# Logits in pairs of blocks, one issue for a chunk's four output products, and a new order of the work

## Chip, core and metric

The kernel runs on one core of a Trainium2 chip. The metric is the device time of one execution in microseconds (us). The kernel before takes 249.48 us, the median of three runs (248.29 to 249.7).

## What is computed

Two stages in fp32. `x` is [4, 11456, 128], `inducing` [32, 128]; the second stage has 8 experts of 4 slots each, 32 slots in all, and a hidden width of 1024.

```python
def mab(q, kv):
    s = scale * (q @ kv.transpose(0, 2, 1))
    s = s - s.max(-1, keepdims=True)
    a = np.exp(s)
    a /= a.sum(-1, keepdims=True) + 1e-09
    return a @ kv
h = mab(I, x)
x = mab(x, h)
...
logits = x @ phi
d = np.exp(logits - logits.max(0, keepdims=True))
d /= d.sum(0, keepdims=True) + 1e-09
slot_input = d.T @ x
...
h = np.maximum(slot_input[e] @ w1[e], 0.0)
slot_out[e] = h @ w2[e]
...
c = np.exp(logits - logits.max(1, keepdims=True))
c /= c.sum(1, keepdims=True) + 1e-09
return c @ slot_out
```

The maxima of `d` run over all 45824 rows of a slot, those of `c` over the 32 slots of a row.

## The kernel before

The rows of a batch are laid out as 128 partitions by 90 blocks, and a **chunk** is 15 blocks: 6 chunks for each of 4 batches, 24 in all (`n` or `a`, 0 to 23). A chunk's working tile is 128 x 480: for each partition, 15 blocks of 32 values. All of the program is a list of steps, each with an engine and a function. A table of numbers, `ORDER`, written out by hand, says in which order the steps are issued; each engine then works through its own in that order and waits where an input or a buffer isn't ready. Costs beside the steps play no part in the running program.

For each chunk the steps are:

- **First pass** (`first_scores`, `first_sum`): TensorE makes the scores `s1p` (L301), VectorE takes a maximum (L312), ScalarE the exponential (L359), VectorE transposes blocks (L362), TensorE sums `ha` (L378). After six chunks a batch's `h` follows from it (`first_out`).
- **Second pass** (`second`): TensorE makes `s2p` (L301), VectorE transposes (L544) and takes row maxima (L547), GpSimd subtracts (L551), ScalarE takes exp (L554), TensorE transposes (`tt`, L560), ScalarE copies (L565, L567), TensorE makes the logits with their row sums, `lp` (L573). VectorE adds 1e-9 to the sums (L582), inverts them (L583) and writes the scaled logits into `l_all` (`ble`, L589); for the last chunk of a batch ScalarE writes the fifteenth block (`blf`, L592). GpSimd scales the weights (L596). `l_all` holds one block after another, 32 slots side by side.
- **Slot maxima** (`segment`, three chunks each, eight segments): for segments 0, 2, 3, 4 and 5 VectorE takes the maximum over three chunks at once (`t`, L630), for the others over one chunk at a time (`tm`, L618). Both walk along the blocks of one slot, 32 values apart. TensorE, VectorE (`mc`, L642), TensorE (`pb`, L645) and ScalarE (`m_all`, L648) spread it over the partitions; GpSimd subtracts it (`d`, L667), ScalarE takes exp (L671), and TensorE adds a chunk's 15 small products to `u` (L680), which ScalarE copies out (L689).
- **Experts** (`experts`): joins the segments (L732 to L757), from which the products `sip` (L748), `sit`, `hpm`, `so` and in the end the matrix `srs` (L844) follow.
- **Third pass** (`third`, with `soft`): row maximum `cm` (VectorE, L483), subtraction `ct` (GpSimd, L487), exp (ScalarE, L491), row sum `cz` (VectorE, L508; where the chunk is in `CHALF`, GpSimd first adds two halves, L499), 1e-9 added (L511, GpSimd for the 18 chunks in `CEP`, VectorE for six), reciprocal (VectorE, L514), scaling (GpSimd, L889), and a transpose back into `l_all` (VectorE, L892). It needs only the logits, so it may run ahead of `srs`; `ct` has three buffers.
- **Output** (`output`): four products for each chunk, one for each group of 32 partitions (L922), each into a bank of its own, taken from six that go round (`mm`); the other two banks belong to `ha` and `u`. ScalarE or VectorE copies each product out (L936), and SyncE's queue stores a chunk (L944).

SyncE's queue also loads `x` in 960 KB pieces into 13 buffers, and at the end the weights.

Of the kernel before, what the change touches and what calls it, by code (L numbers as in the profile page):

```python
# [13 lines left out]
S = 32  # L14
# [14 lines left out]
SZ = S + 1  # L29

# [43 lines left out]

# [973 lines left out]
```

## Time and profile before

| | |
|---|---|
| median of three runs | 249.48 us |
| the profiled execution | 249.23 us |
| its span in the trace | 247.2 us |
| TensorE busy | 206.3 us, 83% |
| VectorE busy | 170.2 us, 69% |
| ScalarE busy | 127.6 us, 52% |
| GpSimd busy | 132.8 us, 54% |
| DMA | 73.86 MB; 23.59 MB of it written |
| mean granted TensorE clock | 0.848 of full |

The span is what the trace covers from the first instruction to the last; the execution's own time is 2.0 us longer. In the rows below PE is TensorE (PEld its weight loads), DVE VectorE, ACT ScalarE, POOL GpSimd, and L12 is line 12 of the kernel. Busy time says how long an engine had an instruction in work, and the idle time before an instruction is put down to what came last.

### The profile page before, as it was taken

The page shows a single profiled execution, that of the slowest core. Times are in us where ns is not written, and L with a number is a line of the kernel's source. Part 1 is how long each engine was busy: PE and PEld are TensorE (multiplying, and loading weights), DVE is VectorE, ACT ScalarE, POOL GpSimd, SP SyncE. Part 2 cuts the span into 40 slices and gives each one's busy share as a digit, 9 for nine tenths or more (in the row PEclk, how much of TensorE's full clock was granted, in tenths as well). Part 3 has the DMA queues.
Part 4 walks back from the last instruction along what each step waited for, and adds up shares of the span by engine and source line. Part 5 has one row for each costly group of instructions (what it writes and reads, how often), then busy time and mean ns, then how long its engine had stood idle before and what let it go on. Part 6 is the DMA issues. An engine that isn't in the chain of part 4 may idle for free.

```text
span 247.2 us, 6831 instructions
## 1 busy us (share of the span) xinstructions
PE 206.3 (83%) x2762; PEld 134.0 (54%) x2762; DVE 170.2 (69%) x389; ACT 127.6 (52%) x307; POOL 132.8 (54%) x155
## 2 busy tenths in 40 slices
PE   7699999999999889979999847898999993849300
PEld 7465654964569753658738737784555460313000
DVE  0123859989999989999999991278895556473400
ACT  3478416662468623767348443035994586545310
POOL 0000004775879569959599889738366126673100
PEclk9999999999999999999999975599995556555555
DMA  7999999979999999939993000001997649297697
GB/s 225 405 427 415 333 414 423 417 326 333 424 418 421 419 416 417 417 111 392 423 419 125 3 0 3 4 3 70 381 416 310 260 179 418 113 415 308 251 401 303
DMA packets 13134, 73.86 MB, mean 299 GB/s; under 512 B 1712, under 2 KB 3376, under 8 KB 13104
## 3 DMA queue, kind: packets, MB, share of 16 engines
q1 hardware_dynamic: 12672, 73.27, 73.4%
q8 instruction: 21, 0.34, 0.6%
q10 hardware_dynamic: 432, 0.17, 0.2%
q14 instruction: 9, 0.07, 0.1%
HBM read 49.84 MB, written 23.59 MB: 297 GB/s over the span
## 4 chain that ended last, share of the span: by engine, by line
PE 50%; DVE 29%; issue 4%; DMA 4%; POOL 4%; ACT 3%; SPq 1%; POOLq 0%; ACTq 0%; DVEq 0%
PE po L922 20%; PE ha L378 7%; PE lp L573 4%; PE s1p L301 4%; DMA xn<-xn 4%; DVE bt L544 4%; DVE tm L618 3%; DVE l_all L589 3%; DVE bm L547 3%; PE tp L278 3%; DVE t L630 3%; DVE l_all L892 3%; PE hpm L802 2%; PE s2p L301 2%; DVE s L312 2%
## 5 line engine op out<-in xcount | busy, mean ns | idle before, releaser
L922 PE MATMUL po<-l_all,srs 32*128 32x480 f32 x192 | 52.2, 872 | 13.0 <-DVE l_all L892 9.8
L936 ACT COPY ot<-po 128x480 f32<-128x480 f32 x71 | 36.3, 568 | 24.3 <-PE po L922 23.6
L922 PEld LDWEIGHTS po<-l_all,srs 32*128 32x128 f32 x192 | 26.1, 258 | 37.8 <-ACT ot L936 18.5
L487 POOL TENSOR_TENSOR ct<-l_all,cm 128x480 f32<-128x480 f32 x24 | 23.8, 995 | 19.5 <-DVE l_all L892 19.2
L551 POOL TENSOR_TENSOR bt<-bt,bm 128x480 f32<-128x480 f32 x24 | 23.6, 998 | 14.5 <-DVE bm L547 12.9
L667 POOL TENSOR_TENSOR d<-l_all,m_all 128x480 f32<-128x480 f32 x24 | 28.7, 1212 | 3.0 <-ACT m_all L648 2.7
L596 POOL TENSOR_TENSOR bt<-bt,bz 128x480 f32<-128x480 f32 x24 | 23.8, 998 | 11.8 <-DVE bz L583 4.8
L936 DVE COPY ot<-po 128x480 f32<-128x480 f32 x25 | 16.0, 646 | 19.7 <-PE po L922 19.7
L889 POOL TENSOR_TENSOR ct<-ct,cz 128x480 f32<-128x480 f32 x24 | 23.8, 996 | 7.8 <-DVE cz L514 3.9
L312 DVE TENSOR_SCALAR_CACHE_REDUCE s<-s1p 128x480 f32<-128x480 f32 (+1 forms) x24 | 15.2, 638 | 16.4 <-PE s1p L301 16.4
L573 PE MATMUL lp<-bdg,a2t 128*128 128x132 f32 x192 | 26.3, 281 | 0.0
L573 PEld LDWEIGHTS lp<-bdg,a2t 128*128 128x128 f32 x192 | 23.4, 190 | 3.7 <-issue 1.8
L378 PE MATMUL ha<-xn,e 128*32 128x128 f32 x570 | 19.8, 275 | 1.8 <-issue 0.9
L301 PE MATMUL s1p<-xt,it_sb 128*32 128x480 f32 x160 | 19.7, 573 | 1.6 <-ACT xt L286 1.1
L671 ACT ACTIVATE d<-d 128x480 f32<-128x480 f32 x24 | 14.3, 605 | 12.9 <-POOL d L667 12.8
L554 ACT ACTIVATE bt<-bt 128x480 f32<-128x480 f32 x24 | 14.3, 604 | 12.5 <-POOL bt L551 12.3
L301 PE MATMUL s2p<-xt,hts 128*32 128x480 f32 x160 | 19.2, 570 | 0.0
L359 ACT ACTIVATE s<-s,negm 128x480 f32<-128x480 f32 (+1 forms) x24 | 16.4, 692 | 5.1 <-DVE negm L343 5.0
L378 PEld LDWEIGHTS ha<-xn,e 128*32 128x32 f32 x570 | 16.0, 109 | 4.3 <-issue 1.7
L491 ACT ACTIVATE ct<-ct 128x480 f32<-128x480 f32 x24 | 14.6, 613 | 5.9 <-POOL ct L487 5.9
L508 DVE TENSOR_REDUCE cz<-ct 128x15 f32<-128x480 f32 x22 | 13.8, 634 | 5.3 <-ACT ct L491 5.3
L892 DVE STREAM_TRANSPOSE l_all<-ct 128x480 f32<-128x480 f32 x24 | 15.7, 664 | 1.6 <-POOL ct L889 1.5
(123 smaller groups left out, 346.7 us busy)
## 6 DMA issues: line engine op xcount, KB each, us to landing
xn<-xn SPq DMA_DIRECT2D x19, 960.0 KB, 10.1
out<-ot SPq DMA_DIRECT2D x19, 960.0 KB, 5.7
xt<-xt SPq DMA_DIRECT2D x14, 960.0 KB, 15.1
w<-w SPq DMA_DIRECT2D x8, 960.0 KB, 8.1
l_all<-xn SPq DMA_DIRECT2D x4, 960.0 KB, 11.5
l_all<-xt SPq DMA_DIRECT2D x4, 960.0 KB, 5.9
out<-ot SPq DMA_DIRECT2D x12, 240.0 KB, 2.5
out<-ot SPq DMA_DIRECT2D x4, 480.0 KB, 5.5
```

Of the source, the lines that this page charges most:

```text
L301: nc.tensor.matmul(dst[32 * g : 32 * g + 32, :w], lhs, src, start=True, stop=True)
L312: nc.vector.tensor_scalar(t[:, :v], T["s1p", a][:, :v], 1.0, None, op0=ALU.mult, op1=ALU.max, accum_out=m6[:, a : a + 1])
L378: nc.tensor.matmul(ha[32 * q : 32 * q + 32, :P], T["e1", a][:, j * S : (j + 1) * S], T["xn", a][:, j * P : (j + 1) * P], start=c == lo and ...
L487: nc.gpsimd.tensor_tensor(blocks(t), blocks(src()), T[mk][:, :nb].unsqueeze(2).broadcast_to(full), op=ALU.subtract)
L551: nc.gpsimd.tensor_tensor(t, t, T["bm", n][:, :nb].unsqueeze(2).broadcast_to(full), op=ALU.subtract)
L573: nc.tensor.matmul(pt[:, q * 4 * SZ : (q * 4 + m) * SZ], t[: m * S, q * P : (q + 1) * P], bdgs[b % 2].rearrange("p q s -> p (q s)")[: m * ...
L596: nc.gpsimd.tensor_tensor(t, t, T["bz", n][:, :nb].unsqueeze(2).broadcast_to(full), op=ALU.mult)
L667: e.tensor_tensor(blocks(t), blocks(l_of(n)), m.unsqueeze(1).broadcast_to([P, nb, S]), op=ALU.subtract)
L889: nc.gpsimd.tensor_tensor(t, t, T["cz", n][:, :nb].unsqueeze(2).broadcast_to([P, nb, S]), op=ALU.mult)
L892: nc.vector.transpose(l_of(n), T[ck][:, :w])
L922: nc.tensor.matmul(ptile(banks[g], po[g])[:, :w], T["srs",][q, :], l_of(n)[q, :], start=True, stop=True)
L936: (nc.vector.tensor_copy if dve else nc.scalar.copy)(ot[:, g * w : (g + 1) * w], T["po", m][:, :w])
```

## The change

**Layout.** `l_all` gives each chunk 16 blocks instead of 15 (`LW` = 512 values), in pairs: the two blocks of a pair lie value by value beside each other, so the two values of one slot are neighbours. The sixteenth block is written with the fifteenth, as its copy. The slot maxima walk over neighbours, then 64 values on to the next pair. What reads or writes single blocks (`ble`, `cm`, most of `ct`) now steps by two values. `blf` runs for all 24 chunks, and `ble` covers 14 blocks.

```diff
 def l_of(n):
-    o = STARTS[n % NCH] * S
-    return l_all[:, n // NCH, o : o + width(n)]
+    return l_all[:, n * LW : n * LW + width(n)]
+def l_pairs(n):
+    return l_all[:, n * LW : (n + 1) * LW].rearrange("p (a s e) -> p a s e", s=S, e=2)
+def l_blocks(n):
+    return l_pairs(n).rearrange("p a s e -> p a e s")
+def l_slots(n, m=1):
+    return l_all[:, n * LW : (n + m) * LW].rearrange("p (a s e) -> p s a e", s=S, e=2)
...
 def mx():
-    nc.vector.tensor_reduce(stile(pre + "m", mk, JM, RINGS[pre + "m"])[:, :nb], blocks(src()), axis=AX.X, op=ALU.max)
+    m = stile(pre + "m", mk, LW // S, RINGS[pre + "m"])
+    nc.vector.tensor_reduce(m.rearrange("p (a e) -> p a e", e=2), l_blocks(n), axis=AX.X, op=ALU.max)
...
-m = nb - (1 if valid(n) < w else 0)
+m = nb - 1
 def ble():
-    z = T["bz", n][:, :m].unsqueeze(2).broadcast_to([P, m, S])
-    nc.vector.tensor_tensor(blocks(l_of(n))[:, :m], lz()[:, :m, :S], z, op=ALU.mult)
+    z = T["bz", n][:, :m].rearrange("p (a e) -> p a e", e=2).unsqueeze(3).broadcast_to([P, m // 2, 2, S])
+    x = lz()[:, :m, :S].rearrange("p (a e) s -> p a e s", e=2)
+    nc.vector.tensor_tensor(l_blocks(n)[:, : m // 2], x, z, op=ALU.mult)
 def blf():
-    nc.scalar.activation(l_of(n)[:, m * S :], lz()[:, m, :S], AF.Identity, scale=T["bz", n][:, m:nb], bias=far)
+    x = lz()[:, m, :S].unsqueeze(2).broadcast_to([P, S, 2])
+    if valid(n) < w:
+        nc.scalar.activation(l_pairs(n)[:, m // 2], x, AF.Identity, scale=T["bz", n][:, m:nb], bias=far)
+    else:
+        nc.scalar.mul(l_pairs(n)[:, m // 2], x, T["bz", n][:, m:nb])
...
-nc.vector.tensor_reduce(T["tm", k][:, i * S : (i + 1) * S], by_slot(l_of(n)), axis=AX.X, op=ALU.max)
+nc.vector.tensor_reduce(T["tm", k][:, i * S : (i + 1) * S], l_slots(n), axis=AX.XY, op=ALU.max)
...
-nc.vector.tensor_reduce(stile("t1", ("t1", k), S, 4), by_slot(l), axis=AX.X, op=ALU.max)
+nc.vector.tensor_reduce(stile("t1", ("t1", k), S, 2), l_slots(ns[0], seg), axis=AX.XY, op=ALU.max)
```

`ds` (the difference `d`) keeps the pairs, and the small products then read `d` in steps of two, except for the four chunks in `DW`, where `ds` itself writes block by block.

**Small steps on other engines.** Both additions of 1e-9 go to ScalarE: 24 times `bze` (from L582) and 24 times `ep` (from L511; `CEP` goes away). Four chunks are subtracted on VectorE instead of GpSimd (`DV = [12, 20, 21, 23]`), and four sums are halved on GpSimd instead of two (`CHALF = [9, 10, 11, 16]`).

```diff
+def bze():
+    nc.scalar.activation(stile("bz", ("bz", n), JM, RINGS["bz"])[:, :nb], lz()[:, :, S], AF.Identity, bias=eps)
 def ep():
-    (nc.gpsimd if slow else nc.vector).tensor_scalar_add(T[zk][:, :nb], T[zk][:, :nb], 1e-9)
+    nc.scalar.activation(T[zk][:, :nb], T[zk][:, :nb], AF.Identity, bias=eps)
```

**Output.** All eight banks go round in one ring (`mm`: 8), and the four products of a chunk are one step of the list. Of the 96 copies VectorE makes 29 instead of 25.

```diff
+def mm():
+    btile("x", ("ot", n))
+    for g in range(4):
+        q = slice(32 * g, 32 * g + 32)
+        nc.tensor.matmul(ptile("mm", ("po", 4 * n + g))[:, :w], T["srs",][q, :], l_of(n)[q, :], start=True, stop=True)
```

**Order.** `ORDER` is a new table throughout, and the costs written beside the steps are other numbers:

```diff
-    "000102030405060e070a08090p0b0c0f0d0h0g0A0l0i0j0q0k0w0m0s0r0u0L0t0n0v0x0B0o0D0C0F0E0W0y0G0H0z0M0I0O170N180Q3o0P0S0J0R0T0X0K0Z0Y113s101319120U1a141f3p0V1i3w1g151l1j3t163q1h3A1b3u1k1c"
+    "000102030406050e07080a090b0p0c0f0d0l0g0h0A0j0i0k0q0m0w0r0s0u0L0t0n0v0x0B0o0D0C0F0E0W0H0G0y0I0M0z0S0N0Q173z180O0J0P0R0X0K0T0Z0Y113D101319120U1a1f3A0V143H1i1g151l1j1h163B1k3L1b1m3E1c"
```

Three places of it. GpSimd ahead of the experts (`d_18` is the difference of chunk 18, `mb` the tile of the joined segments, `bt` a chunk's weights), before:

```order
L667 TENSOR_TENSOR d_18_2269<-l_all_78,m_all_79 128x480
L667 TENSOR_TENSOR d_19_2274<-l_all_78,m_all_79 128x480
L735 TENSOR_TENSOR mb_2214<-m_all_79 128x224
L667 TENSOR_TENSOR d_20_2306<-l_all_78,m_all_79 128x480
L667 TENSOR_TENSOR d_21_2329<-l_all_78,m_all_79 128x480
L667 TENSOR_TENSOR d_22_2351<-l_all_78,m_all_79 128x480
L743 TENSOR_TENSOR mb_2214<-us_all_82,mb_2214 128x224
```

Three differences of chunks 18 to 20 and two of the last segment stand around the two steps on `mb`. GpSimd at the same place now:

```order
L691 TENSOR_TENSOR d_15_2205<-l_all_78,m_all_79 128x512
L691 TENSOR_TENSOR d_16_2220<-l_all_78,m_all_79 128x512
L691 TENSOR_TENSOR d_17_2235<-l_all_78,m_all_79 128x512
L691 TENSOR_TENSOR d_18_2278<-l_all_78,m_all_79 128x512
L691 TENSOR_TENSOR d_19_2300<-l_all_78,m_all_79 128x512
L759 TENSOR_TENSOR mb_2079<-m_all_79 128x224
L620 TENSOR_TENSOR bt_22_2096<-bt_22_2096,bz_22_2222 128x480
L620 TENSOR_TENSOR bt_21_2057<-bt_21_2057,bz_21_2208 128x480
L767 TENSOR_TENSOR mb_2079<-us_all_82,mb_2079 128x224
```

The difference of chunk 20 has left GpSimd for VectorE, and the three of chunks 15 to 17 have come in; two scalings of weights stand between the two steps on `mb`, and chunk 21's and 22's differences don't.

TensorE at the start of the output (`po_29` is product 1 of chunk 7: 29 = 4 x 7 + 1), before:

```order
L922 MATMUL po_0_2623<-l_all_78,srs_83 128x480
L922 MATMUL po_4_2626<-l_all_78,srs_83 128x480
L922 MATMUL po_6_2632<-l_all_78,srs_83 128x480
L922 MATMUL po_7_2635<-l_all_78,srs_83 128x480
L922 MATMUL po_5_2638<-l_all_78,srs_83 128x480
L922 MATMUL po_28_2643<-l_all_78,srs_83 128x480
L922 MATMUL po_2_2648<-l_all_78,srs_83 128x480
L922 MATMUL po_8_2652<-l_all_78,srs_83 128x480
```

Products of chunks 0, 1, 2 and 7 alternate. TensorE at the same place now:

```order
L941 MATMUL po_4_2662<-l_all_78,srs_83 128x480
L941 MATMUL po_5_2664<-l_all_78,srs_83 128x480
L941 MATMUL po_6_2666<-l_all_78,srs_83 128x480
L941 MATMUL po_7_2668<-l_all_78,srs_83 128x480
L941 MATMUL po_0_2674<-l_all_78,srs_83 128x480
L941 MATMUL po_1_2676<-l_all_78,srs_83 128x480
L941 MATMUL po_2_2678<-l_all_78,srs_83 128x480
L941 MATMUL po_3_2680<-l_all_78,srs_83 128x480
```

The four of chunk 1 are followed by the four of chunk 0, and so on, chunk by chunk, to the end.

VectorE late in the output (`l_all<-ct_17` is the transpose that ends the third pass of chunk 17, `ot_16` a copy of chunk 16's output), before:

```order
L936 COPY ot_15_2903<-po_62_2918 128x480
L508 TENSOR_REDUCE cz_17_2926<-ct_17_2872 128x15
L892 STREAM_TRANSPOSE l_all_78<-ct_16_2827 128x480
L514 RECIPROCAL cz_17_2926<-cz_17_2926 128x15
L508 TENSOR_REDUCE cz_18_2939<-ct_18_2900 128x15
L936 COPY ot_16_2936<-po_65_2944 128x480
L514 RECIPROCAL cz_18_2939<-cz_18_2939 128x15
L508 TENSOR_REDUCE cz_19_2956<-ct_19_2934 128x15
L892 STREAM_TRANSPOSE l_all_78<-ct_17_2872 128x480
L892 STREAM_TRANSPOSE l_all_78<-ct_18_2900 128x480
L514 RECIPROCAL cz_19_2956<-cz_19_2956 128x15
L936 COPY ot_17_2962<-po_69_2974 128x480
```

The transpose of chunk 16 stands three rows ahead of the copy of chunk 16's output, and that of chunk 18 two rows ahead of the copy of chunk 17. VectorE late in the output now:

```order
L952 COPY ot_6_2928<-po_25_2931 128x480
L916 STREAM_TRANSPOSE l_all_78<-ct_18_2882 128x480
L526 TENSOR_REDUCE cz_20_2963<-ct_20_2940 128x15
L952 COPY ot_13_2946<-po_53_2949 128x480
L532 RECIPROCAL cz_19_2944<-cz_19_2944 128x15
L952 COPY ot_17_2968<-po_70_2973 128x480
L952 COPY ot_17_2968<-po_69_2971 128x480
L532 RECIPROCAL cz_20_2963<-cz_20_2963 128x15
L526 TENSOR_REDUCE cz_21_3001<-ct_21_2966 128x15
L916 STREAM_TRANSPOSE l_all_78<-ct_19_2901 128x480
L952 COPY ot_16_2987<-po_65_2990 128x480
L532 RECIPROCAL cz_21_3001<-cz_21_3001 128x15
```

The transpose of chunk 19 stands ahead of the copy of chunk 16's output.

## Rows read from the trace of the kernel before

**Rows 1.** by stretch of the span: us, busy us (instructions) of PE, PEld, DVE, ACT, POOL, PEclk, DMA share, GB/s

```profile
53.00:141.00 88.00, 83.46 (x1434) 55.70 (x1432) 85.82 (x192) 48.62 (x134) 69.03 (x72) 1.00 0.84 338
141.00:150.90 9.90, 4.59 (x130) 3.21 (x128) 7.61 (x16) 4.23 (x10) 9.17 (x10) 0.69 0.01 2
150.90:169.10 18.20, 16.74 (x340) 14.53 (x340) 8.34 (x24) 3.28 (x8) 12.39 (x18) 0.70 0.01 3
169.10:203.20 34.10, 33.50 (x127) 19.55 (x128) 23.69 (x47) 25.17 (x52) 16.31 (x20) 0.75 0.71 285
203.20:235.50 32.30, 18.70 (x69) 6.58 (x64) 16.34 (x34) 16.89 (x35) 15.74 (x21) 0.55 0.74 306
```

**Rows 2.** whom TensorE waited for, 53 to 141 us: us in all, times, longest

```profile
PE pt L635 <- DVE negm L343: 1.2, 1, 1.2
PE ha L378 <- issue: 0.9, 1, 0.9
```

**Rows 3.** VectorE's groups, shapes apart: out<-in xcount | busy us, mean ns | idle before

```profile
L582 DVE TENSOR_SCALAR bz<-lp 128x15 f32<-128x15 f32 x24 | 3.6, 148 | 0.9 <-PE lp L573 0.8
L630 DVE TENSOR_REDUCE t<-l_all 128x32 f32<-128x1440 f32 x5 | 13.6, 2722 | 0.0
L618 DVE TENSOR_REDUCE tm<-l_all 128x32 f32<-128x480 f32 x9 | 8.6, 965 | 0.0
L547 DVE TENSOR_REDUCE bm<-bt 128x15 f32<-128x480 f32 x24 | 14.6, 622 | 0.0
L508 DVE TENSOR_REDUCE cz<-ch 128x15 f32<-128x240 f32 x2 | 0.8, 382 | 2.1 <-POOL ch L499 2.1
L508 DVE TENSOR_REDUCE cz<-ct 128x15 f32<-128x480 f32 x22 | 13.8, 634 | 5.3 <-ACT ct L491 5.3
L514 DVE RECIPROCAL cz<-cz 128x15 f32<-128x15 f32 x24 | 5.3, 228 | 0.7 <-POOL cz L511 0.7
L589 DVE TENSOR_TENSOR l_all<-lp,bz 128x480 f32<-128x480 f32 x20 | 12.3, 624 | 0.0
```

**Rows 4.** TensorE's group of the small products u

```profile
L680 PE MATMUL u<-d,bt 128*32 128x32 f32 x720 | 11.5, 210 | 1.2 <-ACT us_all L689 0.9 <-ACT d L671 0.3
```

**Rows 5.** the chain that ended last, 141 to 151 us: start us, us, what

```profile
141.68 0.46 DVE mc L642
...
148.99 0.80 POOL d L667
...
150.14 0.67 POOL mb L743
...
150.86 0.42 PE sip L748
```

**Rows 6.** GpSimd's group of the differences d

```profile
L667 POOL TENSOR_TENSOR d<-l_all,m_all 128x480 f32<-128x480 f32 x24 | 28.7, 1212 | 3.0 <-ACT m_all L648 2.7
```

**Rows 7.** output products on TensorE in order of time: start us, us, line, xcount [idle before]

```profile
169.14 27.76 PE L922 MATMUL po<-l_all,srs 32*128 32x480 f32 x104 [0.44 <-DVE srs L844]
...
216.95 1.98 PE L922 MATMUL po<-l_all,srs 32*128 32x480 f32 x8 [0.97 <-DVE l_all L892]
221.76 7.02 PE L922 MATMUL po<-l_all,srs 32*128 32x480 f32 x24 [2.84 <-DVE l_all L892]
```

**Rows 8.** whom TensorE waited for, 203 to 235 us

```profile
PE po L922 <- DVE l_all L892: 9.8, 4, 3.2
PE po L922 <- DVE cz L514: 2.2, 1, 2.2
```

**Rows 9.** the page's 40 slices: granted TensorE clock in tenths, GB/s moved

```profile
PEclk9999999999999999999999975599995556555555
...
GB/s 225 405 427 415 333 414 423 417 326 333 424 418 421 419 416 417 417 111 392 423 419 125 3 0 3 4 3 70 381 416 310 260 179 418 113 415 308 251 401 303
```

**Rows 10.** ScalarE's groups, shapes apart

```profile
L671 ACT ACTIVATE d<-d 128x480 f32<-128x480 f32 x24 | 14.3, 605 | 12.9 <-POOL d L667 12.8
L592 ACT ACTIVATE l_all<-lp,cst,bz 128x32 f32<-128x32 f32 x4 | 1.5, 379 | 0.8 <-DVE l_all L589 0.8
```

More of the change, by code (lines that the diff above doesn't have):

```diff
@@ L176, in xtile @@
         o = l_end(tag) - XW
-        T[kind, a] = l_all.rearrange("p b s -> p (b s)")[:, o : o + XW]
+        T[kind, a] = l_all[:, o : o + XW]
         return T[kind, a]
@@ L213, in tile_kernel @@
     taken = set()
-    wz = const.tile([P, P], F32, name="wz")
+    wz = T["srs",]
     nc.vector.memset(wz, 0.0)
@@ L250, in load @@
         xw = nb * P
+        assert not {tag_of("xn", a), tag_of("xt", a)} & taken
         def ldn(lo, hi):
@@ L353, in first_sum @@
         lo, hi = groups(b)[g]
-        htag = "ha" if g == len(groups(b)) - 1 else "u"
         nb, w, v = SIZES[c], width(a), valid(a)
@@ L627, in h0 @@
         def h0():
-            o = STARTS[ns[0] % NCH] * S
-            l = l_all[:, ns[0] // NCH, o : o + sum(width(n) for n in ns)]
-            nc.vector.tensor_reduce(stile("t1", ("t1", k), S, 4), by_slot(l), axis=AX.X, op=ALU.max)
+            nc.vector.tensor_reduce(stile("t1", ("t1", k), S, 2), l_slots(ns[0], seg), axis=AX.XY, op=ALU.max)
         def h1():
@@ L650, in segment @@
         if k in TT:
-            op("DVE", dv(sum(width(n) for n in ns)), ("h0", k), h0, [("l", n) for n in ns], [("t1", k)])
+            op("DVE", 0.1 + seg * LW / 930, ("h0", k), h0, [(x, n) for n in ns for x in ("l", "lx")], [("t1", k)])
             op("PE", 0.11, ("h1", k), h1, [("t1", k)], [("pt", k)], [("mm", ("pt", k))], ni=2)
@@ L840, in gf @@
         def gf():
-            nc.tensor.matmul(ptile("ha", ("sr",))[:, :P], rep, T["sos",], start=True, stop=True)
+            nc.tensor.matmul(ptile("mm", ("sr",))[:, :P], rep, T["sos",], start=True, stop=True)
         def gs():
@@ L852, in experts @@
         op("Pool", 0.6, ("e4",), e4, [("ws",), ("mb",)] + [("us", k) for k in range(K)], [("uss",)])
-        op("PE", 0.2 * K, ("e5",), e5, [("uss",), ("mb",)] + [("h", SEG_AT[k] // NCH) for k in range(K)], [("sip",)], [("mm", ("sip",))], ni=4 * K)
+        op("PE", 0.3 * K, ("e5",), e5, [("uss",), ("mb",)] + [("h", SEG_AT[k] // NCH) for k in range(K)], [("sip",)], [("mm", ("sip",))], ni=4 * K)
         op("DVE", 0.3, ("e7",), e7, [("uss",), ("mb",)], [("vs",)])
```

173 lines of the change are left out of this document (85 added, 88 removed).

## The prediction

> **What bounds the kernel now.** I read the busy shares by stretch first, then who waited for whom, then the chain that ended last. The table by stretch [rows 1] shows five parts; the last goes on to 247.2 us. From 53 to 141 us both TensorE (83.46 of 88.0 us) and VectorE (85.82) are busy nearly throughout, and DMA at 0.84. So two engines bound this stretch together: TensorE stands idle for only 4.5 us of it, and what it waited for there is mostly VectorE [rows 2]. From 141 to 150.9 us TensorE is busy for 4.59 us: the last slot maxima and differences run off in a chain. From 150.9 to 169.1 us the experts run, a chain on TensorE. From 169.1 us to the end, 78.1 us, the outputs are stored. The stores are 23.59 MB; the densest slices move 418 GB/s [rows 9], so 56.4 us would do for them, 2.35 us for a chunk, and 21.7 us of this last part are not used by the stores.
>
> The profiled execution took 249.23 us for a span of 247.2; the median of the runs is 249.48. I sum against 249.2. A measurement of this kernel tells a difference from about 0.5% on, 1.25 us.
>
> **The stretch to 141 us: VectorE.** Ahead of the join of the segments VectorE loses, by its groups [rows 3]:
> - 24 additions of 1e-9 at 0.148 us: 3.55 us.
> - The slot maxima. Row sums over adjacent values take 0.634 us for 480 values and 0.382 for 240, so 1.05 ns for a value and 0.13 us fixed. A maximum over 512 adjacent values is then 0.67 us, over three chunks (1536) 1.74. The slot maxima of before, at 32 values' distance, take 0.965 and 2.722 us; by the same fixed part that is 1.74 ns a value. If neighbours in pairs are read like adjacent values, the five large ones save 5 x (2.722 - 1.74) = 4.9 us, and the small ones, nine before and seven now (two come behind the join), 9 x 0.965 - 7 x 0.67 = 4.0 us. If they go on at 1.74 ns, the large ones cost 2.80 us each and the two terms are -0.4 and 1.5. I take the first: the row maxima `bm`, with adjacent values, lie at 0.622 us, and nothing but the step sets them apart from `tm`.
> - One scaling `ble` (0.62) comes behind the join.
>
> It gains a row sum and a reciprocal (0.634 + 0.228), a difference `d` (an operation of two inputs like `ble`, 0.66 for 512 values), and 32 values more in ten `cm` (0.34): 1.9 us. The net is 3.55 + 4.9 + 4.0 + 0.6 - 1.9 = **11.2 us** less, with 3.4 as the other end for the maxima.
>
> `ble` now writes, and `cm` reads, in steps of two values. No row shows such a step. Bounds: nothing, or the 0.69 ns by which a step of 32 exceeds adjacent values: 23 x 448 x 0.69 ns = 7.1 us for `ble` and 10 x 512 x 0.69 ns = 3.5 for `cm`, 10.6 in all, which would leave 0.6 of the 11.2. I take nothing, since two values are nearer to one than to 32; the other end is a rival below.
>
> But TensorE's work stays: as many products of each kind as before. It can give back only the 4.5 us in which it waits, so I count **4.5 us** here, and 11.2 as the far end, if its records look denser than its work is. The products `u` read `d` in steps of two in 20 chunks; a chunk's cost 11.5 / 24 = 0.48 us [rows 4], so between nothing and twice that, 9.6 us. I take nothing, as the nearest row is `u` itself, and keep half for the range.
>
> **The end of this stretch.** From `mc` at 141.68 to `sip` at 150.86 us the chain takes 9.2 us [rows 5]. On it GpSimd makes the differences at 1.21 us each [rows 6]; chunk 20's comes behind the first step on `mb`. Now VectorE makes it. Behind `mc` VectorE has two scalings, three slot maxima, a reciprocal and the join in its queue (2 x 0.62 + 3 x 0.67 + 0.25 + 0.5 = 4.0 us, the join estimated from a 480-value row); then come the difference 0.66, the exponential 0.61, the products 0.65 (0.48 at the mean), a copy and the second step on `mb`, 0.67, together with `mc` some 7.6 us. That is **1.6 us** less. It could be nothing if the two scalings of weights that GpSimd now has ahead of that step come late.
>
> **The experts**, 18.2 us, keep their products and their order but for `zpp`; I count nothing, 2 us either way for the clock, which is granted at 0.70 there [rows 1].
>
> **The output.** Two things change. First the third pass. From 203 us on TensorE waits 12.0 us for it (9.8 for the transposes back, 2.2 behind a reciprocal) [rows 8]; the transposes stood just ahead of the copies of the same chunk in VectorE's queue, and now stand three chunks ahead. GpSimd has also lost 18 small additions and four differences. Second the four products of a chunk. [...] I take 10 of the 12.0 us of waits and 13 x (2.14 - 1.98) = 2 us for the grouping: **12 us** less, to 66 us, 10 above the stores' 56.4. The bounds are nothing and 18: a first group, a copy and the last store's way out, some 4 us, remain above 56.4 in any case.
>
> ScalarE takes 48 additions, and 20 more fifteenth blocks, none dearer than `blf`, 0.379 us [rows 10]: 68 x 0.38 = 26 us at most over the whole kernel. From 53 to 141 us alone it is idle for 39 us [rows 1], so I cost them nothing; if the cover is gone, it is the rival that ends slower. The four copies that VectorE makes in ScalarE's place and the new ring of banks change no engine's work by more than 3 us of 78; I count nothing.
>
> Sum: 249.2 - 4.5 - 1.6 - 0 - 12 = 231.1, so **231 us**.
>
> [...]
>
> **Rivals.**
> 1. *The steps of two are slow on VectorE.* `ble` and `cm` then take back 10.6 of the 11.2 us, VectorE stays the bound to 141 us, and only the output gains: 249.2 - 0.6 - 12 = 237, about 238 with the six `cm` (0.35 each) that are left in the output. For it speaks that every strided row of before is slow, against it only that two is a small step. [...]
> 2. *The output doesn't gain.* The banks come free only as ScalarE copies, and that engine, busy for 25.17 of 34.1 us at the start of the output [rows 1], now also has the additions of the third pass in its queue, behind copies that wait for TensorE. Then 249.2 - 6.1 = 243. Against it: ScalarE's busy time in the last 78 us, 42 us, is far below 66.
> 3. *VectorE waits for ScalarE, and the kernel gets slower.* Up to now VectorE turned `lp` into logits alone. Now each of 24 chunks goes to ScalarE twice, for `bze` ahead of the reciprocal and for `blf` ahead of the maxima, and what stands behind on VectorE waits with it. One hand-over costs up to an exponential in front, 0.605, and its own 0.379 [rows 10], 0.98 us; 48 of them 47 us. From 18 of 47, 38% uncovered, it eats all that I count; at three quarters the kernel takes 249.2 - 18 + 35 = 266. Against it: ScalarE is 45% idle in that stretch, and VectorE's queue has other chunks' work to stand between.
>
> **How the numbers follow.** My forecast, both gains, has 0.62; its own range is 223 (8 and 18 us) to 240 (3 and 6 us). Rival 1 has 0.13, rival 2 0.15, rival 3 0.10. The range reaches from 221, for a first stretch that gains all 11.2, to 244, for rivals 1 and 2 whole, and leaves out rival 3 and the thin ends. Faster by over 0.5%: the forecast, rival 1 and most of rival 2, 0.86. Within 0.5%: the rest of rival 2, 0.04. Slower: rival 3, 0.10.
>
> **What would show it.** Right: slot maxima at 0.67 and 1.74 us, `ble` and `cm` near 0.62 and 0.65; VectorE with idle time before 141 us while TensorE has hardly any; `srs` near 163 us; four products in 2 us or less throughout, and no long waits of TensorE for transposes; stores at 0.85 and more of the last 66 us. Wrong: `ble` at 0.9 us (rival 1), TensorE waiting for ScalarE's copies (rival 2), or VectorE's idle time falling to ScalarE's `bz` and `l_all` (rival 3).

## The result

The changed kernel takes 225.24 us (median of four runs, 224.96 to 225.99), the kernel before beside it 248.88: a ratio of 0.913, with a 95% interval of 0.903 to 0.924. Six more runs of the changed kernel in a later comparison gave 226.01 us, ratio 0.907 (0.903 to 0.910). The forecast was 231 us, with a range of 221 to 244.

The profiled execution of the changed kernel took 225.43 us for a span of 223.3, where the one of before took 249.23 for 247.2. The 23.9 us between the spans divide at four points that both traces show:

| stretch | before | after | difference | forecast |
|---|---|---|---|---|
| to the `mc` ahead of the join of the segments | 141.68 | 135.31 | -6.4 | -4.5 |
| from there to `sip` | 9.2 | 7.3 | -1.9 | -1.6 |
| `sip` to the first output product | 18.3 | 18.1 | -0.2 | 0 |
| first output product to the end | 78.1 | 62.7 | -15.4 | -12 |

The table by stretch, after, against [rows 1] (us, then busy us of TensorE, its weight loads, VectorE, ScalarE and GpSimd with their instructions, granted clock, DMA share, GB/s):

```profile
53.00:135.50 82.50, 81.23 (x1347) 55.37 (x1346) 77.33 (x173) 57.35 (x174) 65.81 (x67) 1.00 0.89 356
135.50:142.60 7.10, 4.31 (x188) 3.33 (x188) 6.92 (x14) 4.64 (x14) 6.88 (x9) 0.82 0.01 2
142.60:160.60 18.00, 16.90 (x370) 14.99 (x370) 11.59 (x31) 5.74 (x14) 15.27 (x18) 0.69 0.01 4
160.60:166.00 5.40, 4.96 (x32) 2.47 (x32) 5.40 (x11) 4.26 (x10) 3.79 (x5) 1.00 0.53 196
166.00:202.20 36.20, 30.85 (x160) 14.75 (x160) 32.45 (x66) 35.28 (x83) 22.80 (x23) 0.99 1.02 413
202.20:223.30 21.10, 0.00 (x0) 0.00 (x0) 0.00 (x0) 0.00 (x0) 0.00 (x0) 0.50 0.87 361
```

In the first row TensorE is now busy for all but 1.3 us, and VectorE, which had 2.2 us idle in 88, has 5.2 in 82.5. The last two rows show an output that the stores set: DMA is full from 166 to 202.2 us (share 1.02, 413 GB/s), and the last 21.1 us are stores alone (0.87, 361 GB/s), when no engine computes any more. ScalarE, which makes most of the copies, is busy for 35.28 of the 36.2 us before that, so it is nearly full too, and the stores are behind it by those 21 us. VectorE's and ScalarE's groups that answer to [rows 3] and [rows 10]:

```profile
L496 DVE TENSOR_REDUCE cm<-l_all 128x16 f32<-128x512 f32 x24 | 15.7, 663 | 0.6 <-POOL ct L505 0.6
L609 DVE TENSOR_TENSOR l_all<-lp,bz 128x448 f32<-128x448 f32 x24 | 14.6, 612 | 0.1
...
L652 DVE TENSOR_REDUCE t<-l_all 128x32 f32<-128x1536 f32 x5 | 8.5, 1709 | 0.0
L642 DVE TENSOR_REDUCE tm<-l_all 128x32 f32<-128x512 f32 x9 | 5.8, 664 | 0.0
...
L598 ACT ACTIVATE bz<-lp,eps 128x15 f32<-128x15 f32 x24 | 6.3, 269 | 4.2 <-PE lp L590 4.0
L616 ACT ACTIVATE l_all<-lp,bz 128x64 f32<-128x64 f32 x20 | 6.2, 319 | 1.2 <-DVE l_all L609 1.1
```

The slot maxima `t` and `tm`, which now read neighbours, went from 2722 and 965 ns to 1709 and 664, though they read more values. `l_all`, which writes in steps of two, and `cm`, which reads so, take about as long for a value (1.37 and 1.29 ns) as `ble` and `bm` do with values side by side (1.30 and 1.30) [rows 3]. What TensorE waits for from 53 to 135.5 us, against [rows 2], is little, and hardly any of it is for VectorE (us in all, times, longest):

```profile
PE s2p L315 <- issue: 1.0, 1, 1.0
PE pm L354 <- DVE m L351: 0.2, 1, 0.2
```

Its two largest waits in the output, from 160 us on, against [rows 8], where the transposes `l_all` alone were 9.8 us:

```profile
PE po L941 <- DVE ot L952: 2.8, 4, 1.2
PE po L941 <- DVE l_all L916: 1.3, 1, 1.3
```

The output products in order of time (start, us, instructions; eight are a chunk's four products), against [rows 7]:

```profile
160.64 4.96 PE L941 MATMUL po<-l_all,srs 32*128 32x480 f32 x32 [0.70 <-DVE srs L868]
166.80 14.81 PE L941 MATMUL po<-l_all,srs 32*128 32x480 f32 x72 [1.21 <-DVE ot L952]
...
199.77 1.09 PE L941 MATMUL po<-l_all,srs 32*128 32x480 f32 x8 [1.30 <-DVE l_all L916]
```

The granted clock in 40 slices of the span, in tenths, against [rows 9]:

```profile
PEclk9999999999999999999999999557999999995555
```

The first four chunks take 4.96 us, 1.24 us each, and the next nine 14.81, 1.65 us each, where before took 2.14 us a chunk at the start. The clock of the output was at half for most of it before (0.75 and 0.55 in the two stretches of [rows 1]); now it is full until the last product (1.00 and 0.99).

### The profile page after: what moved, and what is told of

Same layout as the page of the kernel before. It is cut to its first block, busy times and chain, and to the rows that moved or that the text cites. A ratio compares the mean times of both kernels' runs of the same rounds, so it can differ in the third digit from the quotient of the medians.

```text
span 223.3 us, 6826 instructions
## 1 busy us (share of the span) xinstructions
PE 189.0 (85%) x2762; PEld 126.0 (56%) x2762; DVE 162.1 (73%) x368; ACT 138.1 (62%) x371; POOL 124.9 (56%) x135
## 5 line engine op out<-in xcount | busy, mean ns | idle before, releaser
L941 PE MATMUL po<-l_all,srs 32*128 32x480 f32 x192 | 35.8, 609 | 5.1 <-DVE ot L952 2.8
L952 ACT COPY ot<-po 128x480 f32<-128x480 f32 x67 | 35.1, 679 | 2.8 <-PE po L941 2.8
L941 PEld LDWEIGHTS po<-l_all,srs 32*128 32x128 f32 x192 | 17.2, 183 | 23.1 <-DVE ot L952 10.7
L505 POOL TENSOR_TENSOR ct<-l_all,cm 128x512 f32<-128x512 f32 x20 | 21.0, 1052 | 8.5 <-DVE l_all L916 6.7
L691 POOL TENSOR_TENSOR d<-l_all,m_all 128x512 f32<-128x512 f32 x20 | 22.9, 1166 | 4.4 <-ACT m_all L670 3.2
L391 PE MATMUL ha<-xn,e 128*32 128x128 f32 x600 | 21.0, 275 | 0.0
L509 ACT ACTIVATE ct<-ct 128x480 f32<-128x480 f32 x24 | 15.7, 661 | 6.6 <-POOL ct L505 5.5
L952 DVE COPY ot<-po 128x480 f32<-128x480 f32 x29 | 17.9, 634 | 0.2 <-PE po L941 0.2
L694 ACT ACTIVATE d<-d 128x512 f32<-128x512 f32 x24 | 14.9, 630 | 5.0 <-POOL d L691 2.5
L561 DVE STREAM_TRANSPOSE bt<-s2p 128x480 f32<-128x480 f32 x24 | 15.7, 666 | 1.7 <-PE u L704 0.9
## 6 DMA issues: line engine op xcount, KB each, us to landing
l_all<-xt SPq DMA_DIRECT2D x4, 960.0 KB, 13.5
```

The lines of the kernel that those rows point to most:

```text
L391: nc.tensor.matmul(ha[32 * q : 32 * q + 32, :P], T["e1", a][:, j * S : (j + 1) * S], T["xn", a][:, j * P : (j + 1) * P], start=c == lo and ...
L505: nc.gpsimd.tensor_tensor(t.rearrange("p (a e s) -> p a e s", s=S, e=2), l_blocks(n), m, op=ALU.subtract)
L509: nc.scalar.activation(t, t, AF.Exp)
L691: e.tensor_tensor(t.rearrange(o, s=S, e=2), l_pairs(n), m, op=ALU.subtract)
L941: nc.tensor.matmul(ptile("mm", ("po", 4 * n + g))[:, :w], T["srs",][q, :], l_of(n)[q, :], start=True, stop=True)
L952: (nc.vector.tensor_copy if dve else nc.scalar.copy)(ot[:, g * w : (g + 1) * w], T["po", m][:, :w])
```

## The experiments

All start from the changed kernel, except one that starts from the kernel before. Medians stand beside 225.24 and 226.01 us for the changed kernel and 248.8 to 249.0 for the kernel before.

### What bounds the first stretch now

**Slot maxima far apart again.** The same layout, order and count; only the order in which the maxima walk over it is turned.

```diff
-        return l_all[:, n * LW : (n + m) * LW].rearrange("p (a s e) -> p s a e", s=S, e=2)
+        return l_all[:, n * LW : (n + m) * LW].rearrange("p (a s e) -> p s e a", s=S, e=2)
```

> The slot maxima alone go back to reading values far apart (64 values' distance innermost); layout, order table and all else as in the changed kernel. Both theories: a chunk's maximum near 1.02 us instead of 0.66, three chunks' near 2.80 instead of 1.71, so VectorE has 9 x 0.36 + 5 x 1.09 = 8.7 us more work ahead of 140 us. Theory 'TensorE sets the pace of the first stretch, VectorE has some 5 us of slack in it': about 3.5 us longer, 228 to 229 us, and VectorE busy nearly throughout. Rival 'VectorE still sets the pace': the whole 8.7 us, 233 to 234. Rival 'the order alone made the gain': no more than 1.5 us longer.

Measured: 231.26 us, ratio to the kernel before 0.929 (0.925 to 0.932), 5 to 6 us more than the changed kernel. The two groups of slot maxima:

```profile
L652 DVE TENSOR_REDUCE t<-l_all 128x32 f32<-128x1536 f32 x5 | 14.6, 2914 | 0.0
L642 DVE TENSOR_REDUCE tm<-l_all 128x32 f32<-128x512 f32 x9 | 9.2, 1043 | 0.0
```

The stretch up to the end of the last product `lp`, 139.7 us instead of 135.5, in the columns of the table by stretch:

```profile
53.00:139.70 86.70, 82.53 (x1346) 55.12 (x1345) 85.07 (x172) 56.88 (x175) 66.91 (x68) 1.00 0.85 339
```

The time fell between the two expectations, and the trace says why. The maxima cost 9.4 us more (9 x 0.38 and 5 x 1.21), 0.7 more than priced. Up to the last `lp`, which some of them lie behind, VectorE is busy 7.7 us longer than in the changed kernel (85.07 against 77.33). It took 3.5 of them out of its 5.2 us of idle time, and the other 4.2 are what the last `lp` comes later. VectorE has 1.6 us idle now and TensorE 4.2: VectorE is the bound again. `sip` comes 5.4 us later (148.00 against 142.59). So in the changed kernel VectorE isn't the bound there, but it is only some 4 us from being it again.

**Slot maxima shortened.** The other direction: the maxima read one pair of blocks only, `l_slots(n)[:, :, :1]`, so most of their work is left out.

> The slot maxima read one pair of blocks in place of all (the rest of their work is left out; a smaller maximum only moves the exponentials' scale). VectorE loses another 9 x 0.45 + 5 x 1.4 = 11 us ahead of 140 us. Theory 'TensorE sets the pace there': at most 1.5 us shorter, 223.5 to 225.5 us. Rival 'VectorE still sets the pace': 8 us shorter or more, 217.

Measured: 225.48 us, ratio 0.905 (0.900 to 0.911): no change that can be told. The last `lp` ends 0.6 us sooner, in the columns of the table by stretch:

```profile
53.00:134.90 81.90, 80.99 (x1347) 55.39 (x1345) 68.42 (x173) 56.87 (x174) 65.58 (x67) 1.00 0.90 359
```

VectorE now idles for 13.5 us, TensorE for 0.9. So TensorE is the bound, and work taken off VectorE is worth next to nothing any more.

**The second pass's additions back on VectorE.**

```diff
-            nc.scalar.activation(stile("bz", ...)[:, :nb], lz()[:, :, S], AF.Identity, bias=eps)
+            nc.vector.tensor_scalar_add(stile("bz", ...)[:, :nb], lz()[:, :, S], 1e-9)
```

> The changed kernel, with the addition of 1e-9 ahead of the reciprocal of the second pass back on VectorE (24 of about 0.15 us, 3.55 us, all but some of them ahead of 136 us). Theory 'VectorE has 5.2 us of slack in the first stretch': within 1 us of the changed kernel, 225 to 226.5 us. Rival 'every microsecond on VectorE counts, or the hand-over to ScalarE costs as much as it saves': 228.5 us in the first case, 222 to 224 in the second.

Measured: 227.12 us, ratio 0.910 (0.903 to 0.917), 0.6 us above what the first theory allowed, and not to be told from the changed kernel by the intervals. In the trace the 24 additions take 3.7 us, the last `lp` ends 1.2 us later and `sip` starts 1.85 us later. So some of them count although VectorE has idle time on the whole; the rival (every one counts) asked for 3.5. The other half of the rival, that the hand-over to ScalarE costs as much as it saves, falls: it asked for 222 to 224 us, and in the changed kernel VectorE waits only 2.0 us in all for ScalarE from 53 to 135.5 us.

### What the output's 15 us are

Two things above all had changed there: the third pass is further ahead of the products, and the four products of a chunk stand together. I took them apart both ways. The ring of eight banks and the small steps that left GpSimd came with them, and no run takes these back.

**The kernel before, with the products grouped.** In its order table, the products of a chunk move to the place of the last of them, their copies and stores behind them (chunk, product, on TensorE):

```diff
-po(0,0) po(1,0) po(1,2) po(1,3) po(1,1) po(7,0) po(0,2) po(2,0) po(5,0) ...
+po(1,0) po(1,2) po(1,3) po(1,1) po(0,0) po(0,2) po(0,1) po(0,3) po(5,0) ...
```

> The kernel before, and of the change only this: the four products of a chunk stand together on TensorE, at the place where the last of them stood, and its copies and stores behind them (six banks, as before). The first stretch is untouched. Theory 'the output gains by the third pass's lead and hardly by the grouping': TensorE waits for the transposes as before or more, and the kernel takes 246 to 252 us. Rival 'the grouping itself makes the output's gain': 236 to 240 us. In both a group that doesn't wait takes 1.1 to 1.3 us at full clock.

Measured: 248.61 us, ratio 0.997 (0.993 to 1.001): nothing. The granted clock doesn't stay up by the grouping either: it is 0.97 from 168 to 185 us, 0.55 from 185 to 203 and 0.52 from there to 246. TensorE waits as long for the third pass as in [rows 8], from 168 us to the end:

```profile
PE po L922 <- DVE l_all L892: 9.9, 4, 3.2
PE po L922 <- DVE cz L514: 2.0, 1, 2.0
```

The rival, that the grouping by itself makes the gain, is out. This kernel has six banks, so a second group finds only two of them free while the first is in work; whether the grouping needs the eight isn't shown.

**The changed kernel, with the products mixed again.** Eight banks, the third pass as it is; the products stand in the sequence of the kernel before, a chunk by its place in the order, each followed by its copy (on TensorE, `po(1)` being all four of chunk 1):

```diff
-po(1) po(0) po(10) po(4) ...
+po(1,0) po(0,0) po(0,2) po(0,3) po(0,1) po(10,0) po(1,2) po(4,0) po(3,0) po(10,1) ...
```

> The changed kernel, third pass and its lead untouched, eight banks; only the products of the output stand mixed among the chunks again, in the very sequence of the kernel before (chunk for chunk by its place), each followed by its copy. With the grouping alone in the kernel before having brought nothing, this asks for the other half. Theory 'the lead makes the gain, and a mixed product costs little while the stores bind': TensorE takes some 2 us a chunk, still under a store's 2.35, and the kernel takes 225 to 229 us. Rival 'lead and grouping are worth it only together': 236 us or more, with TensorE or its clock as the limit of the output.

Measured: 232.28 us, ratio 0.934 (0.930 to 0.939), between the two expectations. From the first output product the output takes 69.6 us instead of 62.7. Three stretches of it, in the columns of the table by stretch:

```profile
170.00:180.00 10.00, 9.77 (x36) 4.80 (x28) 7.99 (x18) 8.63 (x20) 6.73 (x8) 0.52 0.77 309
180.00:190.00 10.00, 8.46 (x26) 4.94 (x28) 3.42 (x7) 3.77 (x8) 3.40 (x4) 0.50 0.63 258
190.00:200.00 10.00, 10.00 (x42) 7.71 (x39) 7.67 (x16) 8.34 (x19) 4.76 (x5) 0.50 0.91 374
```

TensorE is as good as always busy in the first and the third, and the clock is at half, where the grouped products of the changed kernel run at 1.00 to 200 us:

```profile
180.00:200.00 20.00, 16.80 (x94) 7.33 (x96) 16.50 (x33) 19.96 (x47) 11.39 (x12) 1.00 1.01 415
```

The stores thin out to 0.63. So the grouping is worth some 7 us, once the third pass is ahead, and nothing in the kernel before. It isn't the mixing as such that takes TensorE longer. Two rows of this run, the first nearly all at half clock (0.52 from 170 to 180 us), the second at full clock (0.94 from 200 to 210 us, the half clock of the stretch before it included):

```profile
169.40 10.37 PE L941 MATMUL po<-l_all,srs 32*128 32x480 f32 x36 [1.32 <-ACT ot L952]
203.48 5.56 PE L941 MATMUL po<-l_all,srs 32*128 32x480 f32 x32 [1.43 <-DVE l_all L916]
```

That is 2.30 us a chunk at half clock, and 1.39 at full, where the changed kernel's groups take 1.24 to 1.65. Nor are the 7 us the clock alone: TensorE waits 7.3 us for the transposes `l_all` here (1.3 in the changed kernel), and VectorE in turn waits 11.0 us with copies for TensorE's products. This run doesn't part the two.

**The third pass as late as it can be.** The changed kernel, products grouped; from the first output product on, third-pass operations are issued only when the next product needs them, so that a chunk's transpose `ctr` stands just ahead of its products:

```diff
-po(8) po(12) ctr(14) po(9) ctr(15) po(7) ctr(16) po(15) po(14) ctr(17) po(6) po(13) ...
+po(8) ctr(12) po(12) po(9) po(7) ctr(13) ctr(14) ctr(15) po(15) po(14) po(6) po(13) ctr(16) ...
```

Counted in groups of products that stand between, chunks 11, 12, 9, 15, 14, 13, 17 and 16 lead by 2, 2, 8, 1, 3, 7, 2 and 5 in the changed kernel, and by 0, 0, 3, 0, 1, 3, 0 and 1 here. The last six, 18 to 23, lead by 4, 0, 1, 1, 1 and 0 there, and by 1 and five times 0 here.

> From the first output product on, the third pass's operations of every queue are issued only where the next product needs them (the transpose just ahead of its chunk's product, as far as that was the order of the kernel before); the group of four stays. Theory 'the lead of the transposes is worth what TensorE waited for them': TensorE waits some 10 us for the transposes again, and the kernel takes 232 to 236 us. Rival 'the stores lag 20 us behind the copies and hide it': TensorE waits as much, but the time stays within 2 us of the changed kernel's.

**And one chunk sooner than that.** The same rule, with leads of 1, 1, 4, 1, 2, 4, 1 and 2, and for the last six of 2 and five times 1.

> As the run in which the third pass's operations come as late as the products allow, but one chunk sooner: the transpose of a chunk is issued one whole chunk ahead of its product. Theory 'the output pays for each part of the third pass's chain that the lead does not cover': clearly between the two, 234 to 243 us, with half of the 29 us of TensorE's waits or less. Rival 'any lead at all is enough': within 2 us of the changed kernel. Rival 'the loss in the late run came from something else than the lead': 248 us or more.

Measured: 251.43 us (ratio 1.013, 1.007 to 1.019), the whole gain of the change lost by an order alone, and far beyond both expectations; and 235.03 us (0.943, 0.939 to 0.946) with one chunk of lead, as its theory had it. TensorE's largest wait in the late run:

```profile
PE po L941 <- DVE l_all L916: 29.1, 8, 5.7
```

VectorE's there, from 170 to 230 us:

```profile
DVE ot L952 <- PE po L941: 16.3, 12, 3.7
```

Two stretches of its output, in the columns of the table by stretch:

```profile
190.00:210.00 20.00, 10.12 (x52) 4.58 (x45) 11.43 (x22) 12.38 (x27) 7.05 (x8) 0.67 0.54 222
210.00:230.00 20.00, 9.90 (x48) 2.96 (x48) 8.53 (x16) 9.74 (x22) 6.05 (x7) 0.59 0.48 197
```

TensorE's largest wait with one chunk of lead:

```profile
PE po L941 <- DVE l_all L916: 12.7, 5, 3.5
```

In these two stretches of the late run no engine is over 62% busy, and DMA is at half. TensorE waits for transposes, and VectorE, which has to make them, waits with copies for TensorE's products: the queues take turns, and no engine is short of time, though TensorE's clock is down to 0.67 and 0.59 as well. The rival, that 20 us of stores in arrears would hide it, fell: the copies come so thinly that the arrears run out. The output takes 88.1 us with no lead, 72.3 with one chunk, 62.7 with the changed kernel's. These runs hold the whole chain back at once, which the kernel before doesn't; that may be why the late run is longer than its 78.1.

| output, from the first product | third pass late | third pass ahead |
|---|---|---|
| products mixed | 78.1 (kernel before) | 69.6 |
| products grouped | 77.8 (before, grouped) | 62.7 (changed kernel) |

The left column has six banks and the right one eight. Eight don't make the gain by themselves: the late run has them too.

**Do the four products run beside each other?** All four read rows 0 to 31 here, so three quarters of the output are other than asked for; number, size and waits are the same.

```diff
-                q = slice(32 * g, 32 * g + 32)
+                q = slice(0, 32)
```

> All four products of a chunk read rows 0 to 31, so that they stand in the same quarter of TensorE's rows (the outputs of three quarters are then other than asked for; instructions, tiles and waits are the same in number and size). Theory 'four different quarters run beside each other, and the group of four is worth it': a product alone takes 0.8 to 0.95 us at full clock, a chunk 3.2 to 3.8 where the changed kernel shows 1.09 to 1.2; TensorE then bounds the output at 77 us or more, and the kernel takes 240 to 253 us. Rival 'the stores set the output's length and the grouping is idle': within 1.5 us of the changed kernel.

Measured: 331.67 us, ratio 1.334 (1.329 to 1.339), far beyond both. The group of the output products:

```profile
L941 PE MATMUL po<-l_all,srs 32*128 32x480 f32 x192 | 151.9, 991 | 0.7 <-DVE srs L868 0.7
```

Two stretches, with TensorE alone (us, busy and instructions, granted clock, DMA share, GB/s):

```profile
160.00:164.00 4.00, 4.00 (x8) 0.74 0.17 61
200.00:260.00 60.00, 60.00 (x76) 0.50 0.35 141
```

96 products in 151.9 us are 1.58 us each, 6.3 a chunk, where [rows 7] show 1.98 us for a group of four at half clock (0.50 granted): the quarters do run beside each other, by a factor of three. At twice the clock that would be, by estimate, the 0.8 us that the expectation had; what it missed is the clock, which fell to half some 2 us after the first product, and stayed at 0.50 from 164 to 310 us, in which TensorE never paused.

### Steps of two, by themselves

The changed kernel, with single operations on 512 values (480 on TensorE) behind its end, one source line for each step: VectorE maxima over steps of 1, 2, 3, 4, 8, 16 (L1002 to L1007), VectorE copies that write so (L1024 on), GpSimd differences that read so (L1014 on), TensorE products that read steps of 1, 2, 4, 16 (L1020 to L1023), ScalarE copies that write steps of 1, 2, 4, 16 (L1036 on).

> The changed kernel with single operations behind its end: VectorE, GpSimd, TensorE and ScalarE read or write 512 values (480 on TensorE) that stand 1, 2, 3, 4, 8 or 16 apart. Theory 'a step of two is free, a larger one is not': on VectorE steps 1 and 2 take the same time to 3%, a step of 16 some 0.35 us (0.69 ns a value) more, reads and writes alike; between, a rise from 3 or from 8 on. Rival 'every step above one is slow, and what the changed kernel shows at a step of two comes from its shape': 0.35 us more from a step of two on. The time of the whole is of no interest.

Measured, in the groups by line (busy us, mean ns of one; TensorE's two instructions are one product):

```profile
L1022 PE MATMUL jp<-l_all,cst 128*128 128x480 f32 x2 | 1.8, 1011 | 0.0
...
L1017 POOL TENSOR_TENSOR jk<-l_all,jk 128x512 f32<-128x512 f32 x1 | 1.2, 1247 | 0.1
...
L1005 DVE TENSOR_REDUCE jk<-l_all 128x1 f32<-128x512 f32 x1 | 1.1, 1131 | 0.0
...
L1038 ACT COPY l_all<-jk 128x512 f32<-128x512 f32 x1 | 1.1, 1091 | 0.0
L1020 PE MATMUL jp<-l_all,cst 128*128 128x480 f32 x2 | 1.1, 618 | 0.0
...
L1015 POOL TENSOR_TENSOR jk<-l_all,jk 128x512 f32<-128x512 f32 x1 | 1.0, 1039 | 0.1
...
L1021 PE MATMUL jp<-l_all,cst 128*128 128x480 f32 x2 | 1.0, 583 | 0.0
...
L1004 DVE TENSOR_REDUCE jk<-l_all 128x1 f32<-128x512 f32 x1 | 0.8, 830 | 0.0
L1002 DVE TENSOR_REDUCE jk<-l_all 128x1 f32<-128x512 f32 x1 | 0.7, 686 | 0.0
L1003 DVE TENSOR_REDUCE jk<-l_all 128x1 f32<-128x512 f32 x1 | 0.7, 676 | 0.0
L1037 ACT COPY l_all<-jk 128x512 f32<-128x512 f32 x1 | 0.6, 646 | 0.0
...
L1027 DVE COPY l_all<-jk 128x512 f32<-128x512 f32 x1 | 0.6, 619 | 0.0
L1036 ACT COPY l_all<-jk 128x512 f32<-128x512 f32 x1 | 0.6, 617 | 27.6 <-POOL l_all L1035 27.6
...
L1025 DVE COPY l_all<-jk 128x512 f32<-128x512 f32 x1 | 0.4, 428 | 0.0
```

A step of two costs within 6% what a step of one costs: VectorE's maxima 676 ns against 686, its writes 428 against 427, GpSimd 1039 against 1038, TensorE 583 against 618, ScalarE 646 against 617. A step of four costs 1.6 to 1.8 times as much in VectorE's maxima, on TensorE and on ScalarE, 1.45 times in VectorE's writes (619), and 1.2 times on GpSimd (1247). The expectation's theory was right on a step of two and off beyond it: four is the dearest step in VectorE's maxima (1131 ns), and a step of 16 adds 0.31 us there and 0.19 in its writes, so reads and writes aren't alike. So rival 1 falls.

### A version that beats both

Between 135 and 143 us TensorE waited 0.28 to 0.83 us several times, the granted clock fell to half at 140 us (0.50 up to 153 us), and `sip` (3.19 us) and most of the experts' first products `hpm` (5.72 us) ran so. Two runs fill these waits with products of the identity, into a bank, or columns of one, that nobody reads; nine of them, of this form:

```diff
             def c2(n=n, i=i, nb=nb):
...
+                if n in {17: 2, 18: 3, 20: 1}:
+                    ptile("mm", ("dm", n))
+                for _ in range({17: 2, 18: 3, 20: 1}.get(n, 0)):
+                    nc.tensor.matmul(T["dm", n][:, :P], ident, ident, start=True, stop=True)
```

with one ahead of a `pb` and two ahead of `sip`.

> The changed kernel with nine products of the identity with itself, into a bank that nobody reads, at the places between 135 and 143 us where TensorE waited (0.28 to 0.83 us each), to keep it busy. Theory 'the clock fell to half at 140 us because of these waits, and the tail and the experts ran at half clock until 153.7 us for that': the granted clock stays full, the sums over segments take 1.6 us instead of 3.2, the experts' first products 3 instead of 5.7, the first output product comes 4 us sooner, and since the stores set the length of the output, the kernel takes 221 to 222 us. Rival 'the clock falls all the same, or what TensorE gains there is waited for elsewhere': 225 us or more.

And the same with three more, ahead of the products of chunks 22 and 23 and of `hpm`:

> As the run with nine products of the identity, and three more behind the sums over segments (one ahead of each of the last two chunks' products, one ahead of the experts' first), where the granted clock fell in that run at 146.7 us. Theory 'it stays full then': the experts' first products take 3.4 us instead of 4.87, and the kernel 1 us less than that run, 222.5 to 223 us at the median. Rival 'the added products delay the chain by as much': 223.8 us or more.

Measured: 223.82 us (ratio 0.899, 0.893 to 0.906), and 223.50 us (0.896, 0.891 to 0.901). The changed kernel itself, run beside the second:

> The changed kernel once more, as the measure for the version beside it: 225.2 us, within 0.5%. By both theories of the other runs the same.

Measured: 226.01 us, 0.907 (0.903 to 0.910). So the twelve products bring 2.5 us at the median, 1.1%, and the intervals of these two lie apart. With nine products the clock fell later, at 146.7 us (0.84 from 146 to 147 us, 0.50 from 147 to 150); with twelve it was 1.00 in every stretch from 139 to 155 us. Both runs lie between their two expectations: the gain is there, and smaller than the theory had it. Whether the filled waits held the clock, or something else in the added products, these runs don't part. The row of the experts' first products with nine, then with twelve:

```profile
146.74 4.87 PE L835 MATMUL hpm<-w,ma 128*32 128x128 f32 x112 [0.34 <-DVE ma L826]
```

```profile
148.69 3.26 PE L838 MATMUL hpm<-w,ma 128*32 128x128 f32 x112
```

A stretch with twelve, with TensorE alone; with nine the clock was 0.50 from 147 to 149 us:

```profile
147.00:149.00 2.00, 1.96 (x50) 1.00 0.00 0
```

`sip` takes 1.75 us in both. From the last `lp` to the first output product it is 21.5 us with twelve (136.94 to 158.44) and 24.5 in the changed kernel beside it (135.49 to 159.95). The first stretch of that profiled run was 1.4 us longer, which no edit explains; so the 3 us are the trace's word, the 2.5 the median's. Whether the second three products add to the first nine can't be told: 0.3 us apart.

## Why the prediction was right, and where its terms were off

**What bounds the first stretch.** That TensorE would take over from VectorE is shown from both sides: 7.7 us more on VectorE made the last `lp` 4.2 later, and shortening the maxima from 14.3 us to 2.5 brought 0.6. The term itself, 4.5 us, measured 6.4. The step that failed is "TensorE's work stays": it gave back its waits (4.5 us idle [rows 1], 1.3 after), and some of its work, about 2 us in busy time, moved behind 135.5 us. [rows 1] had 1434 instructions up to there and 83.46 us busy, now it is 1347 and 81.23, and the next two stretches have 188 and 370 instead of 130 and 340. The rest, under 1 us, is that `mc` no longer comes behind the last `lp`.

**The slot maxima** were forecast at 0.67 and 1.74 us and measured 0.664 and 1.709. The price of one of them at a hop of 64, used in an experiment (1.02 and 2.80), came out at 1.04 and 2.91.

**Steps of two at nothing**: right, by the single operations and by `l_all` and `cm` (612 and 663 ns). The same for the products `u`, 206 ns against 210 [rows 4].

**The end of the stretch**: `mc` to `sip` 7.3 us, forecast 7.6. The difference `d` on VectorE took 0.78 us, not 0.66.

**The output**: forecast 12 us, 10 for the waits and 2 for the grouping; measured 15.4. With the third pass ahead but the products mixed it is 8.5 us less than before, and the grouping brings another 6.9. So the wait term was near, and the grouping term too small by 5 us. The term, 13 x (2.14 - 1.98), sets the 27.76 us of 104 instructions, 13 mixed chunks, against the eight instructions of one group at 216.95 us [rows 7]; no run shows the 2 us that it comes to. The step that failed is the price of a mixed chunk: the 2.14 us are a mean over both clocks, the 1.98 were at half. The 27.76 us, parted where the clock fell, and that group (TensorE alone):

```profile
169.14:185.69 16.55, 16.55 (x75) 1.00 0.84 328
185.69:196.90 11.21, 11.21 (x31) 0.50 0.75 307
216.95:218.93 1.98, 1.98 (x8) 0.50 1.00 407
```

75 instructions in the first part are 1.77 us a chunk, and the other 29 of the 104 (two of the 31 began before) 3.1 us. A mixed chunk at full clock was cheaper than a group at half, 1.98, so the clock was worth at least as much as the grouping. In the changed kernel a group takes 1.24 us at the start, at full clock, and the clock stays up to the last product (1.00 from 160.6 to 200.86 us); in the run with mixed products it was down from 170 to 201 us (0.52, 0.50 and 0.50 in the three stretches to 200). So the 5 us that the term lacked came with the clock and with the waits for transposes in that run, and how they divide is open. Grouping alone doesn't keep the clock: it fell too in the kernel before with grouped products (0.55 from 185 to 203 us), and in the late run (0.59 to 0.67 in the stretches from 170 to 230). That the two gains also need each other (grouping alone brought nothing) was not in the sum at all. The upper bound of 18 us and the floor from the stores held: 62.7 us against 56.4 + 4. The lead wasn't three chunks throughout, as I wrote: counted in groups of products it is none to eight for the chunks from 9 on, and chunk 19's transpose still stands just ahead of its products.

**The sum.** All four stretches gained more than forecast, by 1.9, 0.3, 0.2 and 3.4 us, so no miss made up for another. The lower bound of the range, 221, doesn't come out of the terms shown: 249.2 - 11.2 - 18 is 220.

**The rivals.** Steps of two were free. The output did gain. ScalarE didn't set its length, since the stores took longer still. But it was busy for 35.28 of 36.2 us up to the last copy, so that rival was closer than its "far below 66" says. The slower end, VectorE waiting for ScalarE, was priced at 35 us and came to 2.0 from 53 to 135.5 us; that other chunks' work covers the rest is argued, not shown.

## What to carry to other kernels

Before you shorten the work on one of two engines that are both busy, look at how idle the other is: that, and little more, is what can come back (here 4.5 us idle, 6.4 back), and one added-work and one left-out-work run show which of them binds. In a stage that ends in stores, count how many chunks the work ahead of the products leads by: here, for eight chunks in the middle, leads of one to eight against none to three were worth 26 us of 225, as much as the whole change. And keep small products that sit in different quarters of TensorE's rows next to each other (here worth 6.9 us with the third pass ahead, nothing without), and try filling its short waits on a serial chain (here 2.5 us at the median): read a price per chunk only within one clock (here 1.77 us for a mixed chunk at full clock, 3.1 at half), since the clock is part of the price of an order.

## What the runs showed of the hardware that I had not expected

- The granted clock fell to half while TensorE's records leave no gap: 0.50 over 60.00 us of 60.00 busy when all products sat in the same quarter of the rows, and 0.50 to 0.52 at 9.77 and 10.00 of 10 us busy when quarters came mixed among chunks; 1.00 with the four quarters together and less busy time (16.80 us in the 20 from 180 us on). So a busy TensorE in the records didn't hold the clock here. Nor did mixed products always lose it: they ran at 1.00 up to 185.69 us in the kernel before, and for the first 10 us in the run with mixed products. What exactly holds it, these runs don't settle.
- Idle times of at most 0.83 us each, in a stretch of very small products, went ahead of the fall at 140 us, and with products of no use in these places, some 3 us of them, it stayed at 1.00 up to 146.7 us.
- A step of three values costs in between: in VectorE's maxima 830 ns, where 686 and 1131 stand for one and four, and in its writes 0.51 us, where 0.43 and 0.62 stand for two and four.
